# Low parts on VectorE, high parts by way of PSUM: one edit to the back phase of a fused attention and two-MLP kernel

## The chip, the core and the metric

The kernel runs on one core of a Trainium2 chip. The metric is the device time of one execution in microseconds (us), the median of three runs. Five engines work side by side: TensorE (PE, with its weight loads PEld), VectorE (DVE), ScalarE (ACT), GpSimd (POOL) and SyncE (SP), whose queue issues all the transfers here. Each works through its own instructions in order and waits for the others by semaphores.

## The reference

Windowed attention over (4, 8, 576, 64) gives 2304 tokens of width 512; two MLPs follow. The edit touches the second MLP only.

```python
def _moe_ref(x, w_in, w_out):          # first MLP, d_ff 2048
    h = x @ w_in
    g = h * np.cos(h)
    return (g @ w_out).astype(np.float32)

def _moe2_ref(x, w_a, w_b, w_out):     # second MLP, d_ff 1536
    a = x @ w_a
    b = x @ w_b
    return (a * b @ w_out).astype(np.float32)
```

## The kernel before, in words

**Precision.** Each fp32 operand is split in two: a high part, an ACT copy into the type that PE takes, and a low part, the fp32 value minus the high part, made by DVE or POOL. `mm3` then issues three matmuls: high by high (L430), high by low (L431), low by high (L432).

**The second MLP** runs after the attention and the first MLP. The 2304 tokens go in three groups (`GROUPS`) of 768. Each product of matrices is done as a 2x2 block scheme with seven block products P1 to P7 instead of eight. Its operand on the token side is one of seven blocks, named in `RHS`: P1 takes B11, P6 takes T2, P2 takes B21, P7 takes T3, P5 takes T1, P4 takes T4, P3 takes B22. T1 to T4 are sums of blocks and are made by POOL (`g_sum` for the back phase, `x_sum` for the projections). A group has 126 items, counted by `k`; `q` is its place in the group.

- **Projections**, q = 0 to 83: six pairs p of columns, 14 items each (P1, P6 for `a`, the same for `b`, P2, P7 for `a`, ... in the list `prods`). An item is two `mm3`, six matmuls of 384 columns. Results stand in PSUM banks `z`; DVE adds them up, multiplies `a` by `b` and leaves the blocks B11 to B22 in tiles `g` and `gp`.
- **Back phase**, q = 84 to 125 (r = q - 84 = 0 to 41): `a*b` times `w_out`. The seven products come in the order P1, P6, P2, P7, P5, P4, P3, six items each, so P1 is r = 0 to 5, P6 is 6 to 11, P2 is 12 to 17. Every item needs the high and low part of one block of `a*b` (`gh`, `gl`). `split_g(k + LG)` writes them into the queues LG = 6 items ahead of their use.

**What sets the order.** The main loop over `k` issues, in this order: weight loads (`fetch`), splits of the weights six items ahead (`stage`, tiles `sb`), `split_g`, the tasks of `xitems` (loads, sums and splits of the next group's input, tiles `xb`, `xh`, `xl`, `xw`, `xq`), the tasks of `soon` (`g_sum` and others), then the item itself. `InOrder` keeps ACT, DVE and POOL in the order of writing. So a late sum in POOL's queue holds up what stands behind it in ACT's and in DVE's.

**Which engine makes a low part** in the back phase is in the table `GDS`, one number for each product: (3, 3, 0, 2, 2, 3, 3) sends every third, every third, none, every second, ... to POOL, 14 of the 42 items of a group.

**PSUM** has eight banks in two sets of four, the tags `att`, `h` and `acc0` to `acc3`. `banks()` hands out the sets in turn: one to each pair of the projections, one to the back phase. During the back phase the other set is idle.

**`ev()`** hands out eight SBUF buffers in a ring for intermediate sums; `pair()` takes one of the 33 buffers `w` that the weight loads use as well. In the profile all instructions that `InOrder` records, that is all of the second MLP on ACT, DVE and POOL, have line L64.

Of the kernel before, what the change touches and what calls it, by code (L numbers as in the profile page):

```python
# [9 lines left out]
F32 = mybir.dt.float32  # L10
F32R = mybir.dt.float32r
# [4 lines left out]
AF = mybir.ActivationFunctionType  # L16
ALU = mybir.AluOpType
# [3 lines left out]
NT, DM = B * S, H * D  # L21
# [34 lines left out]


class InOrder:
    def __init__(self, tc, engine):
        self.tc, self.engine = tc, engine  # L60

    def __getattr__(self, name):
        f = getattr(self.engine, name)
        return lambda *a, **k: self.tc.keep_in_program_order(f(*a, **k))  # L64


@with_exitstack
def kernel(ctx, tc, qT, kT, vw, vds, w_in, w_out, w_a, w_b, w_out2, out):
    nc = tc.nc
    pe, act, dve, pool, sp = nc.tensor, nc.scalar, nc.vector, nc.gpsimd, nc.sync  # L70
# [5 lines left out]
    ps = ctx.enter_context(tc.tile_pool(name="ps", bufs=1, space=bass.MemoryType.PSUM))  # L76
# [350 lines left out]
    acc = {}  # L427
# [86 lines left out]
    if True:  # L514
# [181 lines left out]
        def x_sum(nm, j):  # L696
            if nm == "T3":
                t23 = pair("xb")
                xs["T2", j], xs["T3", j] = t23[:, 0], t23[:, 1]
            a, b = {"T3": ("B22", "T1"), "T1": ("T1", "B11"), "T2": ("B22", "T1"), "T4": ("B21", "T2")}[nm]  # L700
            pool.tensor_tensor(out=xs[nm, j], in0=xs[a, j], in1=xs[b, j], op=ALU.subtract)

        def x_hi(nm, j):
            if nm in ("B11", "T2", "T4", "B22"):
# [14 lines left out]

        J2 = [0, 1]  # L720
        xsteps = {5: [(load_x, 0, j) for j in J2]}
        for i, nm in ((7, "T3"), (8, "T1"), (9, "T2"), (12, "T4")):
            xsteps.setdefault(i, []).extend((x_sum, nm, j) for j in J2)
        for i, nm in ((8, "B11"), (9, "B21"), (10, "T3"), (11, "T1"), (12, "T2")):
            for f, at_ in ((x_hi, i), (x_lo, i + 1)):
                xsteps.setdefault(at_, [])[:0] = [(f, nm, j) for j in J2]
        xitems = {}
        for i, (nm, j) in enumerate([("T4", 0), ("T4", 1), ("B22", 0), ("B22", 1)]):
            xitems.setdefault((0, 1 + i), []).append((x_hi, nm, j))
            xitems.setdefault((0, 2 + i), []).append((x_lo, nm, j))  # L730

        def x_plan(G, r0):
            for j in J2:
                xitems.setdefault((G - 1, r0 - 14 + j), []).append((load_x, G, j))
                for r, nm in ((2, "T3"), (14, "T1"), (18, "T2"), (24, "T4")):
                    xitems.setdefault((G - 1, r0 + r + 2 * j), []).append((x_sum, nm, j))
                for r, nm in ((-6, "B11"), (-2, "B21"), (2, "B22"), (8, "T3"), (20, "T1"), (24, "T2"), (30, "T4")):
                    xitems.setdefault((G - 1, r0 + r + 2 * j), []).append((x_hi, nm, j))
                    xitems.setdefault((G - 1, r0 + r + 2 * j + 1), []).append((x_lo, nm, j))

        p2 = None
        for g in range(NG + LAG):
            if g < NG:
                i, u, f = seq[g]
                if g == NG - NF:
                    at_ctx.close()
                    p2 = ctx.enter_context(tc.tile_pool(name="p2", bufs=1))
                    act, dve, pool = InOrder(tc, act), InOrder(tc, dve), InOrder(tc, pool)
# [52 lines left out]
        def split_g(k):  # L801
            if k >= len(items) or items[k][0] != "back":
                return
            _, G, what, p = items[k]
            t = gt[RHS[what], p]
            r = k % PERI - NPR
            for d, tag in ((gh, "gh"), (gl, "gl")):
                if r % 2 and r < NP * len(AB) - 8:
                    d[k] = p2.tile([128, N2], F32R, tag="sb", name=tag, bufs=8)
                else:  # L810
                    d[k] = tmp.tile([128, N2], F32R, tag=tag, name=tag, bufs=C["NGH"])
            act.activation(out=gh[k], in_=t, func=AF.Copy)
            every = C["GDS"][AB.index(what)]
            (pool if every and p % every == every - 1 else dve).tensor_tensor(out=gl[k], in0=t, in1=gh[k].bitcast(F32), op=ALU.subtract)
            if what == "P2":
                gt["T4", p] = t
                soon.setdefault(k - LG + 2, []).append((g_sum, "T4", "B21", "T2", p))

        zlast = [None]
        seg = [0]  # L820

        def banks():
            s = seg[0] % 2
            seg[0] += 1
            names = (("att", 2), ("h", 2)) * 2 if s == 0 else tuple((f"acc{m}", 1) for m in range(4))
            return [ps.tile([128, N2], F32, tag=tag, name="z", bufs=n) for tag, n in names]

        def gtile(nm, p):
            if nm in ("B12", "B22"):
                gt[nm, p] = p2.tile([128, N2], F32, tag="g2", name="g2", bufs=12)  # L830
            else:
# [11 lines left out]
        def product(k, G, p, i):  # L843
# [40 lines left out]
            if not own and done:  # L884
                a = st["a"][done]
                dve.tensor_tensor(out=a, in0=a, in1=c[done], op=ALU.mult)
            if not own and what == "P3":
                gt["T1", p] = gt["B12", p]
                for d, nm, x, y in ((3, "T3", "B22", "T1"), (4, "T1", "T1", "B11"), (5, "T2", "B22", "T1")):
                    soon.setdefault(k + d, []).append((g_sum, nm, x, y, p))  # L890

        def g_sum(nm, x, y, p):
            dst = gt[nm, p] if nm in ("T1", "T4") else gtile(nm, p)
            pool.tensor_tensor(out=dst, in0=gt[x, p], in1=gt[y, p], op=ALU.subtract)

        def put(G, m, h, t):
            s0 = GROUPS[G] + N2 * h
# [61 lines left out]
        for k, it in enumerate(items):  # L959
# [78 lines left out]
```

## Time and profile before

| | |
|---|---|
| median of three runs | 988.29 us (987.73 to 989.37) |
| the profiled execution | 987.76 us, of which 985.6 us lie between its first and last instruction (the span) |
| PE, PEld busy | 942.4 us (96%), 892.4 us (91%) |
| DVE, ACT, POOL busy | 708.1 us (72%), 609.9 us (62%), 477.5 us (48%) |
| granted TensorE clock, mean | 0.979 of full speed |

The profiled execution is 0.53 us below the median. A sum that is made against the profile is therefore raised by that to be compared with a median. PE's busy time is modelled (its matmuls overlap), so what an item costs is better read from the distance of starts.

### The profile page before, as it was taken

How to read it: one execution, taken by the hardware profiler on the slowest of the kernel's cores; microseconds unless marked ns; L12 is line 12 of the kernel's file. 1: busy time of each engine (PE TensorE's matmuls, PEld its weight loads, DVE VectorE, ACT ScalarE, POOL GpSimd, SP SyncE). 2: the span in 40 equal slices, each digit the busy share in tenths (PEclk: the TensorE clock that was granted, in tenths of full speed). 3: DMA queues.
4: the chain of work that ended last, by engine and by line, in shares of the span. 5: the costliest groups of instructions: out<-in, count | busy, mean ns of one | idle time of the engine just before them, and what ended most of it. 6: DMA issues, size and time to landing. Idle time of an engine off the chain costs nothing.

```text
span 985.6 us, 18933 instructions
## 1 busy us (share of the span) xinstructions
PE 942.4 (96%) x6828; PEld 892.4 (91%) x6828; DVE 708.1 (72%) x1378; ACT 609.9 (62%) x1399; POOL 477.5 (48%) x615
## 2 busy tenths in 40 slices
PE   4888899999999999999999999999999999999998
PEld 3767898989889989899999989998999998999998
DVE  7677777577767777656346878889856789667773
ACT  5689897476675858676468765555444455444452
POOL 3757642014221351112015347658777769566682
PEclk8779999999999999999999999999999999999999
DMA  9646511244546363432049855576554685753431
GB/s 287 244 132 209 189 43 39 69 126 138 157 125 184 116 185 113 123 105 60 1 138 280 253 181 193 188 288 238 222 173 154 205 340 214 256 176 141 160 134 49
DMA packets 98829, 163.30 MB, mean 166 GB/s; under 512 B 6960, under 2 KB 64816, under 8 KB 98736
## 3 DMA queue, kind: packets, MB, share of 16 engines
q1 hardware_dynamic: 98736, 162.10, 49.7%
q8 instruction: 54, 0.88, 0.4%
q14 instruction: 39, 0.32, 0.1%
HBM read 128.25 MB, written 33.82 MB: 164 GB/s over the span
## 4 chain that ended last, share of the span: by engine, by line
PE 73%; DVE 10%; ACT 6%; DMA 5%; POOL 4%; issue 2%; SPq 0%; POOLq 0%; DVEq 0%; ACTq 0%
PE z L431 12%; PE z L432 12%; PE z L430 12%; PE h L430 5%; PE acc L430 5%; PE h L431 5%; PE h L432 5%; PE acc L432 5%; PE acc L431 5%; DMA vs<-in_vds_dram 2%; PE att L336 2%; PE att L217 1%; PE att L244 1%; POOL vd L183 1%; PE att L329 1%
## 5 line engine op out<-in xcount | busy, mean ns | idle before, releaser
L64 POOL TENSOR_TENSOR sb<-w,sb 128x256 fp32r<-128x256 f32 x154 | 120.7, 796 | 90.7 <-ACT sb L64 87.0
L430 PE MATMUL h<-xh,w 128*128 128x288 f32 (+1 forms) x448 | 146.7, 327 | 7.9 <-DVE gs L478 7.0
L430 PE MATMUL acc<-gh,w 128*128 128x288 f32 (+1 forms) x448 | 145.0, 325 | 2.0 <-DVE ev L463 1.0
L431 PE MATMUL acc<-gl,w 128*128 128x288 f32 (+1 forms) x448 | 142.3, 318 | 1.9 <-POOL gl L486 1.7
L432 PE MATMUL h<-xh,w 128*128 128x288 f32 (+1 forms) x448 | 142.1, 317 | 1.2 <-POOL w L126 1.2
L431 PE MATMUL h<-xl,w 128*128 128x288 f32 (+1 forms) x448 | 142.9, 319 | 0.0
L432 PE MATMUL acc<-gh,w 128*128 128x288 f32 (+1 forms) x448 | 141.9, 317 | 0.0
L64 ACT ACTIVATE sb<-w 128x256 fp32r<-128x256 f32 x252 | 96.4, 415 | 66.1 <-PE z L432 54.2
L430 PEld LDWEIGHTS h<-xh,w 128*128 128x128 f32 x448 | 85.6, 191 | 15.5 <-DVE gs L478 9.9
L432 PE MATMUL z<-xh,sb 128*128 128x384 f32 x288 | 97.4, 338 | 0.2 <-POOL sb L64 0.2
L430 PE MATMUL z<-xh,sb 128*128 128x384 f32 x288 | 96.9, 336 | 0.4 <-issue 0.4
L431 PE MATMUL z<-xl,sb 128*128 128x384 f32 x288 | 97.2, 338 | 0.0
L430 PEld LDWEIGHTS acc<-gh,w 128*128 128x128 f32 x448 | 85.1, 190 | 7.7 <-issue 2.9
L618 POOL TENSOR_TENSOR praw<-praw 128x128 f32<-128x128 f32 x24 | 12.8, 531 | 162.3 <-DVE praw L118 128.5
L431 PE MATMUL z<-gl,w 128*128 128x384 f32 x252 | 85.7, 340 | 4.4 <-DVE gl L64 4.1
L431 PEld LDWEIGHTS acc<-gl,w 128*128 128x128 f32 x448 | 85.2, 190 | 4.0 <-POOL gl L486 2.1
L432 PEld LDWEIGHTS h<-xh,w 128*128 128x128 f32 x448 | 86.0, 192 | 2.8 <-POOL w L126 1.5
L431 PEld LDWEIGHTS h<-xl,w 128*128 128x128 f32 x448 | 85.8, 192 | 1.9 <-issue 0.9
L432 PEld LDWEIGHTS acc<-gh,w 128*128 128x128 f32 x448 | 85.0, 190 | 2.4 <-issue 1.1
L430 PE MATMUL z<-gh,w 128*128 128x384 f32 x252 | 85.1, 338 | 0.1
L432 PE MATMUL z<-gh,w 128*128 128x384 f32 x252 | 84.9, 337 | 0.0
L64 DVE TENSOR_TENSOR sb<-w,sb 128x256 fp32r<-128x256 f32 x98 | 62.2, 637 | 26.5 <-ACT sb L64 26.4
(141 smaller groups left out, 2503.6 us busy)
## 6 DMA issues: line engine op xcount, KB each, us to landing
w<-wd SPq DMA_DIRECT2D x63, 512.0 KB
w<-wd_a SPq DMA_DIRECT2D x18, 512.0 KB
w<-wd_b SPq DMA_DIRECT2D x18, 512.0 KB
raw<-in_w_in_dram SPq DMA_DIRECT2D x16, 512.0 KB
raw<-in_w_out_dram SPq DMA_DIRECT2D x16, 512.0 KB
w<-wd_a SPq DMA_DIRECT2D x18, 384.0 KB
w<-wd_b SPq DMA_DIRECT2D x18, 384.0 KB
praw<-in_w_a_dram SPq DMA_DIRECT2D x12, 512.0 KB
```

The costliest lines, as they stand in the source:

```text
L64: return lambda *a, **k: self.tc.keep_in_program_order(f(*a, **k))
L183: pool.tensor_tensor(out=o, in0=t[:, :, 0], in1=t[:, :, 1], op=ALU.add)
L217: pe.matmul(p[r, W * w:W * w + W], qt[u, hp][r, off:off + W], kt[b, hp][r, BASE[half] + off:BASE[half] + off + W], start=not pem, stop=True,)
L244: pe.matmul(p[a][:QD, :SD], qd[u, hp][r, :], kd[b, hp][r, :], start=True, stop=True)
L329: pe.matmul(p[64 * a:64 * a + 64, NB:NB + QD], vdt[b, hp][:, a, c], pd[u, hp][:, 2 * a + c], start=(c == 0), stop=(c == 1),)
L336: pe.matmul(p[64 * a:64 * a + 64, xo:xo + n], vt[u, hp // 2][r, w, a], pt[u, hp // 2][r, w, 64 * a + qo:64 * a + qo + n], start=True, stop ...
L430: i = pe.matmul(ps_out, lh, rh, start=start, stop=False, skip_group_check=more)
L431: pe.matmul(ps_out, lh, rl, start=False, stop=False, skip_group_check=more)
L432: pe.matmul(ps_out, ll, rh, start=False, stop=stop, skip_group_check=more)
L618: pool.tensor_tensor(out=s1, in0=a21, in1=a22, op=ALU.add)
```

## The change

**In the back phase** `GDS` goes: DVE makes all low parts of P6 to P3, 36 for each group. For odd p (up to r = 38, which makes 16 for each group) ACT first copies the high part into a PSUM bank of the idle set (tile `hq`), and DVE subtracts that instead of the copy in SBUF. The matmuls take `gh` from SBUF as before.

**P1's splits move.** Its operand B11 is complete in the projections after P2 of `b`. It now stands in an `ev()` buffer, and its high and low part are made two and three items later (`b11_hi`, `b11_lo`) into a pair `gq`; for odd p POOL makes the low part, for even p DVE.

**The sums are ordered anew.** T2 is T3 + B11 instead of B22 - T1, so it comes before T1. Those of the last pair follow 1, 2 and 3 items after their last input instead of 3, 4 and 5. **The next group's input** is loaded at r = 0 instead of r = -14, its sums stand at r = 14 to 32 instead of 2 to 26, and its splits run from r = 6 to 47, the last ones in the next group's projections (before: -6 to 33). `InOrder` is written in another way and keeps the same order.

```diff
+SUMS = {"T3": ("B22", "T1", ALU.subtract), "T2": ("T3", "B11", ALU.add), "T1": ("T1", "B11", ALU.subtract),
+        "T4": ("B21", "T2", ALU.subtract)}
...
-                xitems.setdefault((G - 1, r0 - 14 + j), []).append((load_x, G, j))
-                for r, nm in ((2, "T3"), (14, "T1"), (18, "T2"), (24, "T4")):
-                for r, nm in ((-6, "B11"), (-2, "B21"), (2, "B22"), (8, "T3"), (20, "T1"), (24, "T2"), (30, "T4")):
+                put_x(G - 1, r0 + j, load_x, G, j)
+                for r, nm in ((14, "T3"), (18, "T2"), (24, "T1"), (30, "T4")):
+                for r, nm in ((6, "B11"), (12, "B21"), (24, "T2"), (28, "T3"), (33, "T1"), (39, "B22"), (44, "T4")):
...
+            if what == "P1":
+                gh[k], gl[k] = gsplit[p]
+                return
...
             act.activation(out=gh[k], in_=t, func=AF.Copy)
-            every = C["GDS"][AB.index(what)]
-            (pool if every and p % every == every - 1 else dve).tensor_tensor(out=gl[k], in0=t, in1=gh[k].bitcast(F32), op=ALU.subtract)
+            hi = gh[k].bitcast(F32)
+            if p % 2 and r < NP * len(AB) - 3:
+                tag, n = BANKS[seg[0] % 2][nst[1] % 4]
+                nst[1] += 1
+                hi = ps.tile([128, N2], F32, tag=tag, name="hq", bufs=n)
+                act.copy(out=hi, in_=gh[k].bitcast(F32))
+            dve.tensor_tensor(out=gl[k], in0=t, in1=hi, op=ALU.subtract)
...
+                if done == 11:
+                    soon.setdefault(k + 2, []).append((b11_hi, p))
+                    soon.setdefault(k + 3, []).append((b11_lo, p))
             if not own and what == "P3":
                 gt["T1", p] = gt["B12", p]
-                for d, nm, x, y in ((3, "T3", "B22", "T1"), (4, "T1", "T1", "B11"), (5, "T2", "B22", "T1")):
+                for d, nm in ((3, "T3"), (4, "T2"), (5, "T1")) if p < NP - 1 else ((1, "T3"), (2, "T2"), (3, "T1")):
...
+        def b11_hi(p):
+            q = pair("gq", F32R)
+            gsplit[p] = q[:, 0], q[:, 1]
+            act.activation(out=q[:, 0], in_=gt["B11", p], func=AF.Copy)
+
+        def b11_lo(p):
+            hi, lo = gsplit[p]
+            (pool if p % 2 else dve).tensor_tensor(out=lo, in0=gt["B11", p], in1=hi.bitcast(F32), op=ALU.subtract)
```

What POOL does around the start of the first group's back phase, before the change: the sums of the last pair of columns (`gp<-g,g` T3, `g<-g,gp` T1, `gp<-g,g` T2) stand among low parts `gl` and sums `xb` for the next group.

```order
L64 TENSOR_TENSOR gl<-gp,gh 128x384 x3
L64 TENSOR_TENSOR xb<-xb 128x384
L64 TENSOR_TENSOR gp<-g_8395,g_8343 128x384
L64 TENSOR_TENSOR g_8343<-g_8343,gp 128x384
L64 TENSOR_TENSOR xb<-xb 128x384
L64 TENSOR_TENSOR gp<-g_8395,g_8343 128x384
L64 TENSOR_TENSOR gl<-gp,gh 128x384
L64 TENSOR_TENSOR gp<-gp 128x384 x5
```

The same place of POOL's queue after the change (`gp<-gp,ev` is T2 = T3 + B11, `gq` the low part of B11 for the last pair, `gp<-gp` the six sums T4):

```order
L938 TENSOR_TENSOR gq<-ev,gq 128x384
L929 TENSOR_TENSOR gp<-g_8405,g_8352 128x384
L929 TENSOR_TENSOR gp<-gp,ev 128x384
L929 TENSOR_TENSOR g_8352<-g_8352,ev 128x384
L929 TENSOR_TENSOR gp<-gp 128x384 x6
L717 TENSOR_TENSOR xb<-xb 128x384 x8
```

All low parts have left POOL; T2 is the second of three sums that follow one another, and the sums for the next group stand behind all of the block sums.

DVE at the same place before the change: adds and multiplies of the last pair (`z`, `g`, `gp`), low parts, and low parts for the next group's input (`xl`, `xw`), mixed.

```order
L64 TENSOR_TENSOR gl<-gp,gh 128x384
L64 TENSOR_TENSOR g_8343<-g_8343,z 128x384
L64 TENSOR_TENSOR xw<-xb,xw 128x384
L64 TENSOR_TENSOR z<-ev,z 128x384
L64 TENSOR_TENSOR g_8343<-g_8343,z 128x384
L64 TENSOR_TENSOR gl<-gp,gh 128x384 x2
L64 TENSOR_TENSOR xw<-xb,xw 128x384
L64 TENSOR_TENSOR gl<-gp,gh 128x384
L64 TENSOR_TENSOR xl<-xb,xh 128x384
```

And after it, from the same multiply on:

```order
L872 TENSOR_TENSOR g_8352<-g_8352,z 128x384
L872 TENSOR_TENSOR z<-ev,z 128x384
L917 TENSOR_TENSOR g_8352<-g_8352,z 128x384
L842 TENSOR_TENSOR gl<-gp,gh 128x384
L842 TENSOR_TENSOR gl<-gp,hq 128x384
L842 TENSOR_TENSOR gl<-gp,gh 128x384
L842 TENSOR_TENSOR gl<-gp,hq 128x384
```

The low parts that follow the last multiply are now P6's, every second one with the PSUM operand `hq`; P1's and the next group's are gone from between the adds.

ACT at the same place after the change; a copy `hq` stands behind every second `gh`, and the two copies `ev<-z` wait for PE's end of P1:

```order
L934 ACTIVATE gq<-ev 128x384
L835 ACTIVATE gh<-gp 128x384 x2
L841 COPY hq<-gh 128x384
L835 ACTIVATE gh<-gp 128x384 x2
L841 COPY hq<-gh 128x384
L835 ACTIVATE gh<-gp 128x384 x2
L841 COPY hq<-gh 128x384
L963 COPY ev<-z 128x384 x2
```

Before it, `xh` and `xw` for the next group's input stood in the place of the copies `hq`.

## Rows read from the trace of the kernel before

**Rows 1.** Busy time by stage: projections and back phase of the three groups.

```profile
575.70:665.65 89.95, 89.08 (x505) 88.47 (x505) 77.13 (x138) 50.84 (x126) 58.39 (x71) 1.00 0.57 202
665.65:713.16 47.51, 45.22 (x253) 44.00 (x253) 44.72 (x54) 24.35 (x55) 38.03 (x32) 1.00 0.63 233
713.16:801.57 88.41, 88.41 (x506) 88.41 (x505) 61.61 (x113) 41.76 (x107) 64.20 (x79) 1.00 0.62 210
801.57:849.12 47.55, 45.25 (x253) 44.08 (x253) 44.71 (x54) 24.35 (x55) 38.05 (x32) 1.00 0.58 210
849.12:937.72 88.60, 88.60 (x506) 88.60 (x505) 61.63 (x114) 40.66 (x103) 57.40 (x71) 1.00 0.54 191
937.72:982.12 44.40, 44.40 (x253) 44.08 (x252) 25.86 (x36) 18.74 (x38) 24.82 (x21) 1.00 0.21 80
```

**Rows 2.** PE's waits in these stages: us in total, times, longest.

```profile
PE z L431 <- DVE gl L64: 4.1, 4, 1.3
PE z L431 <- POOL gl L64: 0.3, 2, 0.2
```

**Rows 3.** PE in order of time, first back phase: the two long waits.

```profile
683.55 0.44 PE L431 MATMUL z<-gl,w 128*128 128x384 f32 x1 [0.71 <-DVE gl L64]
...
687.55 0.44 PE L431 MATMUL z<-gl,w 128*128 128x384 f32 x1 [1.32 <-DVE gl L64]
```

**Rows 4.** ACT in order of time, ahead of these waits.

```profile
675.25 0.53 ACT L64 ACTIVATE gh<-gp 128x384 fp32r<-128x384 f32 x1 [5.23 <-POOL gp L64]
```

**Rows 5.** POOL in order of time, ahead of that wait of ACT.

```profile
668.47 1.34 POOL L64 TENSOR_TENSOR xb<-xb 128x384 f32<-128x384 f32 x1
670.07 1.27 POOL L64 TENSOR_TENSOR gp<-g,g 128x384 f32<-128x384 f32 x1 [0.26 <-DVE g L64]
...
672.59 1.34 POOL L64 TENSOR_TENSOR xb<-xb 128x384 f32<-128x384 f32 x1
673.89 1.33 POOL L64 TENSOR_TENSOR gp<-g,g 128x384 f32<-128x384 f32 x1
```

**Rows 6.** DVE in order of time in the first back phase.

```profile
667.62 1.32 DVE L64 TENSOR_TENSOR xw<-xb,xw 128x384 fp32r<-128x384 f32 x1
...
669.44 0.55 DVE L64 TENSOR_TENSOR g<-g,z 128x384 f32<-128x384 f32 x1
...
682.13 1.83 DVE L64 TENSOR_TENSOR gl<-gp,gh 128x384 fp32r<-128x384 f32 x2
683.88 1.37 DVE L64 TENSOR_TENSOR xw<-xb,xw 128x384 fp32r<-128x384 f32 x1
685.18 1.00 DVE L64 TENSOR_TENSOR ev<-ev,z 128x384 f32<-128x384 f32 x2
```

**Rows 7.** One low part of DVE and one of POOL, each without the other.

```profile
707.69 0.56 DVE L64 TENSOR_TENSOR gl<-g,gh 128x384 fp32r<-128x384 f32 x1 [0.90 <-ACT gh L64]
...
706.64 1.02 POOL L64 TENSOR_TENSOR gl<-g,gh 128x384 fp32r<-128x384 f32 x1 [3.07 <-ACT gh L64]
```

**Rows 8.** DVE's groups of the first back phase: busy us, mean ns.

```profile
L64 DVE TENSOR_TENSOR gl<-gp,gh 128x384 fp32r<-128x384 f32 x18 | 18.3, 1053 | 0.0
...
L64 DVE TENSOR_TENSOR ev<-ev,z 128x384 f32<-128x384 f32 x9 | 4.6, 545 | 0.8 <-PE z L432 0.8
```

**Rows 9.** POOL's groups of the first back phase.

```profile
L64 POOL TENSOR_TENSOR xb<-xb 128x384 f32<-128x384 f32 x8 | 10.6, 1331 | 0.0
L64 POOL TENSOR_TENSOR gl<-gp,gh 128x384 fp32r<-128x384 f32 x7 | 8.8, 1255 | 2.8 <-ACT gh L64 2.8
```

**Rows 10.** ACT's groups of the first back phase.

```profile
L64 ACT ACTIVATE gh<-gp 128x384 fp32r<-128x384 f32 x22 | 10.7, 522 | 11.3 <-PE z L432 5.6 <-POOL gp L64 5.2 <-PE z L431 0.4
...
L64 ACT COPY ev<-z 128x384 f32<-128x384 f32 x4 | 1.8, 476 | 2.3 <-PE z L432 2.2
```

**Rows 11.** Busy time at the start of the second group's projections.

```profile
713.20:728.00 14.80, 14.80 (x86) 14.80 (x85) 8.55 (x18) 6.61 (x17) 10.01 (x14) 1.00 0.40 120
```

**Rows 12.** PE in order of time, first projections: P5 of `b`, first pair.

```profile
586.53 0.44 PE L430 MATMUL z<-xw,sb 128*128 128x384 f32 x1 [0.67 <-DVE gp L64]
```

In Rows 1 and 11 the columns are: the stretch in us from the span's start, its length, then for PE, PEld, DVE, ACT and POOL the busy us and (x) the number of instructions, the granted clock, the share of the transfer engines and GB/s. In rows in order of time they are: start and duration in us, engine, line, operation, output and inputs, and in brackets the idle time before it and what ended that.

More of the change, by code (lines that the diff above doesn't have):

```diff
@@ L58, with __init__, written, settle @@
 class InOrder:
[L59 to L64, printed above, removed]
+    def __init__(self, tc, engines):
+        self.tc = tc
+        self.last = {e.engine: None for e in engines}
+        self.seen = len(self.written())
+    def written(self):
+        return self.tc.nc.cur_bb.bb.instructions
+    def settle(self):
+        for ins in self.written()[self.seen:]:
+            if ins.engine in self.last:
+                if self.last[ins.engine] is not None:
+                    self.tc.add_manual_dep(
+                        ins, self.last[ins.engine],
+                        mybir.DependencyInfo(mybir.DependencyClass.NoSync, mybir.DependencyReason.DATA),
+                        reason="program order")
+                self.last[ins.engine] = ins.name
+        self.seen = len(self.written())
 @with_exitstack
@@ L699, in x_sum @@
                 xs["T2", j], xs["T3", j] = t23[:, 0], t23[:, 1]
-            a, b = {"T3": ("B22", "T1"), "T1": ("T1", "B11"), "T2": ("B22", "T1"), "T4": ("B21", "T2")}[nm]
-            pool.tensor_tensor(out=xs[nm, j], in0=xs[a, j], in1=xs[b, j], op=ALU.subtract)
+            a, b, op = SUMS[nm]
+            pool.tensor_tensor(out=xs[nm, j], in0=xs[a, j], in1=xs[b, j], op=op)
         def x_hi(nm, j):
@@ L721 @@
         xsteps = {5: [(load_x, 0, j) for j in J2]}
-        for i, nm in ((7, "T3"), (8, "T1"), (9, "T2"), (12, "T4")):
+        for i, nm in ((7, "T3"), (8, "T2"), (9, "T1"), (12, "T4")):
             xsteps.setdefault(i, []).extend((x_sum, nm, j) for j in J2)
-        for i, nm in ((8, "B11"), (9, "B21"), (10, "T3"), (11, "T1"), (12, "T2")):
+        for i, nm in ((8, "B11"), (9, "B21"), (10, "T3"), (11, "T2"), (12, "T1")):
             for f, at_ in ((x_hi, i), (x_lo, i + 1)):
@@ L747 @@
                     p2 = ctx.enter_context(tc.tile_pool(name="p2", bufs=1))
-                    act, dve, pool = InOrder(tc, act), InOrder(tc, dve), InOrder(tc, pool)
+                    order = InOrder(tc, (act, dve, pool))
                 h_mm(g, u, f)
@@ L812, in split_g @@
             act.activation(out=gh[k], in_=t, func=AF.Copy)
-            every = C["GDS"][AB.index(what)]
-            (pool if every and p % every == every - 1 else dve).tensor_tensor(out=gl[k], in0=t, in1=gh[k].bitcast(F32), op=ALU.subtract)
+            hi = gh[k].bitcast(F32)
[5 more added lines that the diff above has]
+            dve.tensor_tensor(out=gl[k], in0=t, in1=hi, op=ALU.subtract)
             if what == "P2":
                 gt["T4", p] = t
-                soon.setdefault(k - LG + 2, []).append((g_sum, "T4", "B21", "T2", p))
+                soon.setdefault(k - LG + 2, []).append((g_sum, "T4", p))
         zlast = [None]
         seg = [0]
+        BANKS = ((("att", 2), ("h", 2)) * 2, tuple((f"acc{m}", 1) for m in range(4)))
         def banks():
@@ L824, in banks @@
             seg[0] += 1
-            names = (("att", 2), ("h", 2)) * 2 if s == 0 else tuple((f"acc{m}", 1) for m in range(4))
-            return [ps.tile([128, N2], F32, tag=tag, name="z", bufs=n) for tag, n in names]
+            return [ps.tile([128, N2], F32, tag=tag, name="z", bufs=n) for tag, n in BANKS[s]]
         def gtile(nm, p):
@@ L830, in gtile @@
                 gt[nm, p] = p2.tile([128, N2], F32, tag="g2", name="g2", bufs=12)
+            elif nm == "B11":
+                gt[nm, p] = ev()
             else:
@@ L886, in product, with g_sum @@
                 dve.tensor_tensor(out=a, in0=a, in1=c[done], op=ALU.mult)
+                if done == 11:
+                    soon.setdefault(k + 2, []).append((b11_hi, p))
+                    soon.setdefault(k + 3, []).append((b11_lo, p))
             if not own and what == "P3":
                 gt["T1", p] = gt["B12", p]
-                for d, nm, x, y in ((3, "T3", "B22", "T1"), (4, "T1", "T1", "B11"), (5, "T2", "B22", "T1")):
-                    soon.setdefault(k + d, []).append((g_sum, nm, x, y, p))
-        def g_sum(nm, x, y, p):
+                for d, nm in ((3, "T3"), (4, "T2"), (5, "T1")) if p < NP - 1 else ((1, "T3"), (2, "T2"), (3, "T1")):
+                    soon.setdefault(k + d, []).append((g_sum, nm, p))
+        def g_sum(nm, p):
+            x, y, op = SUMS[nm]
             dst = gt[nm, p] if nm in ("T1", "T4") else gtile(nm, p)
-            pool.tensor_tensor(out=dst, in0=gt[x, p], in1=gt[y, p], op=ALU.subtract)
+            pool.tensor_tensor(out=dst, in0=gt[x, p], in1=gt[y, p], op=op)
+        def b11_hi(p):
[5 more added lines that the diff above has]
+            (pool if p % 2 else dve).tensor_tensor(out=lo, in0=gt["B11", p], in1=hi.bitcast(F32), op=ALU.subtract)
+        gsplit = {}
         def put(G, m, h, t):
@@ L979 @@
                 back2(k, *it[1:])
+        order.settle()
 _INS = ["qT", "kT", "vw", "vds", "w_in", "w_out", "w_a", "w_b", "w_out2"]
```

11 lines of the change are left out of this document (7 added, 4 removed).

## The prediction

> **What bounds the kernel now.** I read the stages of the second MLP first. The six stretches of [rows 1] are projections and back phase of three groups that do the same matmuls. The first two back phases take 47.51 and 47.55 us, the third 44.40. In the third PE has no gap: 252 matmuls in 44.40 us are 0.176 us each, the step of the gapless projections too (504 in 88.41). The first two are thus 3.11 and 3.15 us too long, 6.26 together, and this is what an edit of the back phase can win. The third group has no next input to prepare, and DVE is busy 25.86 us in it against 44.72 and 44.71.
>
> PE's waits say what is late: low parts, 4.1 us of them DVE's in four waits and 0.3 POOL's [rows 2]; the restart of the matmul pipeline behind each gap makes up the rest of the 6.26. The two long waits of the first group end at 683.55 and 687.55 [rows 3]. The second group repeats them at the same distance from its start, so nothing random is in it.
>
> Why a low part is late is read from the queues ahead of it. ACT sat 5.23 us until 675.25 behind a POOL sum [rows 4]. That sum is T2 of the last pair. POOL reached it last of three, after low parts and with two sums `xb` for the next group between: T3 at 670.07, an `xb` at 672.59, T2 at 673.89 [rows 5]. DVE then had a train of low parts at double price. One alone took 0.56 us, one of POOL alone 1.02 [rows 7]; while both engines run, the same forms take 1.3 to 1.4 on either [rows 6, 9], and DVE's mean in the phase is 1053 ns [rows 8]. DVE's adds with one PSUM operand keep to 545 ns in the same phase [rows 8]. So two engines that each read two SBUF tiles get in each other's way, and a PSUM operand takes DVE out of it.
>
> **The change part by part.** Prices: two adds in a row took 1.00 us, one alone 0.55, so DVE's step is 0.45 to 0.47 us; I use 0.47. The `xw` at 683.88 was followed by the next instruction at 685.18, a step of 1.30 [rows 6]. A collision thus costs DVE about 0.82 us.
>
> *DVE in the first two back phases.* By the new order it has there 36 low parts, 11 low parts of the next input, 13 adds and multiplies and 2 weight splits: 62 instructions, 29.1 us at 0.47. POOL has 3 + 6 block sums and 8 sums `xb`, 17 in all. No POOL instruction can hit more than about one of DVE's, so collisions add at most 17 x 0.82 = 13.9: 43.0 us, under the 44.4 that PE needs. As a cross-check, before it is 54 instructions: 25.4 us, and the measured 44.72 leaves 19.3, that is 24 collisions with POOL's 32 instructions [rows 1]. Of the 62, 16 low parts and the 13 adds and multiplies read PSUM; I expect some 10 collisions, 37 us. In the third group DVE gets 12 low parts more and P1's fewer, POOL keeps 9 sums, and DVE had 18.5 us to spare [rows 1].
>
> For `hq` as an operand the trace has no low part. The adds (545 ns, one PSUM operand) and the lone low part (0.56, two SBUF operands) are the nearest rows [rows 7, 8], and they agree, so 0.47 stands. [...]
>
> *The first waits.* The multiply that ended at 669.99 on DVE stood behind an `xw` [rows 6]; without it, and leaving P1's low parts uncounted, it ends by 668.75. Up to the low part that PE missed first (r = 16, wanted at 682.5, just ahead of [rows 3]) DVE now has 11 low parts, 5 of them with `hq`, and 2 of the next input. If all eight that read SBUF alone collide: 8 x 1.29 + 5 x 0.47 = 12.7, ready at 681.4, still in time; POOL has far fewer than eight instructions to run there. ACT must have T2's high part by then. POOL's three sums now follow one another from about the same input, at 1.27 to 1.33 each [rows 5], so T2 is ready about 670 to 671 instead of 675.2. Behind that, each low part is queued six items ahead, 6 x 6 x 0.176 = 6.3 us.
>
> *ACT* gets 16 copies `hq` for each group. No row shows ACT writing PSUM. Nearest are 476 ns from PSUM to SBUF and 522 from SBUF to SBUF [rows 10]; in a train the 55 instructions of the phase averaged 0.44 [rows 1]. I take 0.5 and keep 0.4 to 0.8. In the 36 items in which splits are made (38 us) ACT has 50 other instructions, 22 us, so a copy may cost up to 1.0 us before ACT is the bound. Each copy stands ahead of the next `gh`; the first also waits until DVE has emptied the other bank set, which it does with the multiplies that the low parts follow anyway.
>
> *P1's splits* are 6 high parts on ACT and 6 low parts for each group, before and after. Before, they were issued in the last six items of the projections, 4 low parts to DVE and 2 to POOL; now each follows its pair of columns, 3 and 3. DVE has 27 us to spare in the second and third, 12.8 in the first [rows 1]. Their cover is the gap of two or three items between a DVE result and PE's next use of the bank. Without cover each costs 0.47 to 1.29; for the nine on DVE that is 4.2 to 11.6 us. I take 0.3 for all, since the first group is tight at its start, where PE already waits 0.67 us for DVE's multiply [rows 12], and `gq` stands behind that multiply.
>
> *The next input.* Four low parts (B22, T4) now fall into the first items of the next projections, at most 4 x 1.29 = 5.2 us on DVE, which was busy 8.55 of 14.80 there [rows 11]; T4 is first wanted ten items in, five after its low part. Its loads are issued some 15 items later but still 6 ahead of the first split, with the transfer engines at 0.63 [rows 1]. Both are costed at nothing; a miss would cost about 1 us for each boundary, 2 in all. The order of T2 and T1 and the form of `InOrder` cost nothing: the number of sums stays.
>
> **Sum.** -6.26 + 0.3 = -5.96 against the profiled 987.76: 981.8. That execution is 0.53 below the median, so 982.3 for a median. PE, with its unchanged matmuls, remains the bound.
>
> **The rivals.**
> *Only half goes.* From r = 34 on all high parts share one ring of four buffers, so the lead falls from six items to three or four (3.2 us), and DVE has three low parts of the next input there. If PE waits there, or the second long wait stays, about half is won: 988.3 - 3.1 = 985.2. Against it: that shortage was there before too, and no wait of [rows 3] lies there; POOL is idle then.
> *Nothing goes.* The change might not do what it says: if `hq` did not keep DVE clear of POOL and ACT came late by the copies, the waits would move from r = 16 to other items: 988.0. The bound of 43.0 does not need `hq` at all, which speaks against it.
> *Slower.* P1's low parts on DVE come out in the open in the projections, at the hand-over from DVE's reading a bank to PE's reusing it, as once in [rows 12]. With 1.29 each for nine, 988.3 - 6.3 + 11.6 = 993.6; slower from 0.7 us each on. Against it: only the first group shows such a wait, and only one, with DVE at 77.13 of 89.95 us; the others have DVE at 61.6 of 88.5 [rows 1].
>
> **How the numbers follow.** The forecast has 0.76, half 0.09, nothing 0.09, slower 0.06. About 0.2% (2 us) is what a measurement of this kernel tells from no change. Half is still faster by 0.3%: faster 0.85, same 0.09, slower 0.06. The forecast's own range runs from 980.8 (all of the 6.26 and the wait of [rows 12] and its like in the first projections, another 1.2) to 984 (the 2 us at the boundaries); to hold eight in ten I take it up to the half case, 986.
>
> **What would show it.** Right: the first two back phases last 44.4 to 45 us with no wait of `z` for `gl` over 0.3; DVE is busy 35 to 41 us in each; low parts with `hq` take 0.55 beside a busy POOL; copies `hq` take 0.4 to 0.6; T2 of the last pair is done by 671. The projections stay within 0.5 us of [rows 1]. Wrong: PE waiting for DVE `ev` or `gq` inside the projections, for ACT `hq` ahead of a low part, or for `xl` at the start of a group; or `hq` copies over 1 us.

## The result and the profile after

| | before | after |
|---|---|---|
| median of 10 runs | 989.15 us (984.14 to 993.35) | 979.94 us (977.28 to 985.18) |
| ratio after to before | | 0.991, 95% interval 0.988 to 0.993 |
| the profiled execution, its span | 987.76, 985.6 us | 977.28, 975.4 us |

The change is faster by 0.9%. The median lies 2.4 us below the forecast of 982.3 and 0.9 us below the range. The ten runs of before have a median 0.86 us above that of the three runs that the forecast started from, so the medians differ by 9.2 us where the forecast had 6.0.

The stages of the second MLP after the change (columns as in [rows 1]):

```profile
572.86:661.86 89.00, 88.82 (x504) 88.50 (x505) 72.85 (x138) 49.23 (x123) 59.76 (x72) 1.00 0.59 208
661.86:706.04 44.18, 44.18 (x254) 44.18 (x254) 35.59 (x58) 32.74 (x73) 23.33 (x21) 1.00 0.62 232
706.04:794.63 88.59, 88.59 (x505) 88.59 (x505) 65.46 (x118) 40.58 (x106) 66.95 (x80) 1.00 0.62 216
794.63:838.75 44.12, 44.12 (x253) 44.12 (x253) 35.57 (x58) 32.79 (x73) 23.31 (x20) 1.00 0.59 221
838.75:927.25 88.50, 88.50 (x505) 88.50 (x505) 64.54 (x118) 41.84 (x106) 60.03 (x72) 1.00 0.51 179
927.25:971.59 44.34, 44.34 (x253) 44.01 (x252) 25.96 (x47) 26.16 (x54) 10.64 (x9) 1.00 0.30 115
```

Against [rows 1] the first two back phases are 3.33 and 3.43 us shorter, and PE has no gap left in them: 252 matmuls in 44.18 us are 0.1753 us each, the step of the projections before (504 in 88.41). The third phase gained 0.06. The projections changed by -0.95, +0.18 and -0.10. The six stages together lost 7.68 us (406.41 to 398.73, from the first matmul's start). The second MLP also began earlier, at 572.86 instead of 575.72 (2.86 us), behind code that the change leaves alone but for the order of a few of the first group's input sums and splits close to its end.

PE's waits for the second MLP after the change, all that the view lists:

```profile
PE z L444 <- issue: 0.4, 1, 0.4
PE z L446 <- POOL sb L819: 0.2, 1, 0.2
```

The waits for `gl` of [rows 2] are gone. The groups of DVE and ACT in the first back phase:

```profile
L842 DVE TENSOR_TENSOR gl<-gp,gh 128x384 fp32r<-128x384 f32 x12 | 11.2, 936 | 1.7 <-ACT gh L835 1.7
L842 DVE TENSOR_TENSOR gl<-gp,hq 128x384 fp32r<-128x384 f32 x12 | 6.6, 546 | 3.2 <-ACT hq L841 3.2
...
L872 DVE TENSOR_TENSOR ev<-ev,z 128x384 f32<-128x384 f32 x8 | 4.0, 546 | 0.0
...
L835 ACT ACTIVATE gh<-gp 128x384 fp32r<-128x384 f32 x22 | 11.3, 520 | 4.3 <-PE z L446 1.9 <-POOL gp L929 1.9 <-DVE gl L842 0.4
L841 ACT COPY hq<-gh 128x384 f32<-128x384 f32 x16 | 7.7, 484 | 5.2 <-DVE g L872 4.7
```

A low part that reads `hq` takes 546 ns, to the nanosecond what the adds with a PSUM operand take; with `gh` the mean of these twelve is 936. DVE and POOL in order of time, where both are busy:

```profile
679.41 1.37 DVE L842 TENSOR_TENSOR gl<-gp,gh 128x384 fp32r<-128x384 f32 x1
680.70 0.54 DVE L842 TENSOR_TENSOR gl<-gp,hq 128x384 fp32r<-128x384 f32 x1
...
677.74 10.39 POOL L717 TENSOR_TENSOR xb<-xb 128x384 f32<-128x384 f32 x8
```

The hand-over from the projections, phase start 661.86: DVE's last multiply of the last pair, POOL's T3 and T2, and ACT's wait for T2.

```profile
662.66 0.55 DVE L917 TENSOR_TENSOR g<-g,z 128x384 f32<-128x384 f32 x1
...
663.29 1.26 POOL L929 TENSOR_TENSOR gp<-g,g 128x384 f32<-128x384 f32 x1 [6.09 <-DVE g L917]
664.63 1.22 POOL L929 TENSOR_TENSOR gp<-gp,ev 128x384 f32<-128x384 f32 x1
...
665.88 0.53 ACT L835 ACTIVATE gh<-gp 128x384 fp32r<-128x384 f32 x1 [1.90 <-POOL gp L929]
```

Counted from the start of the phase, the multiply ends at 1.35 us (before at 4.34 [rows 6]), T2 at 3.99 (before at 9.57 [rows 5]).

### The profile page after: what moved, and what is told of

It is laid out like the page before. It is cut to its first block, busy times and chain, and to the rows that moved or that the text cites. A ratio compares the mean times of both kernels' runs of the same rounds, so it can differ in the third digit from the quotient of the medians.

```text
span 975.4 us, 18988 instructions
## 1 busy us (share of the span) xinstructions
PE 937.6 (96%) x6828; PEld 890.0 (91%) x6828; DVE 692.2 (71%) x1411; ACT 632.3 (65%) x1447; POOL 440.2 (45%) x582
## 4 chain that ended last, share of the span: by engine, by line
PE 77%; DVE 7%; ACT 6%; DMA 4%; POOL 3%; issue 3%; SPq 0%; DVEq 0%; POOLq 0%; ACTq 0%
PE z L446 14%; PE z L445 14%; PE z L444 14%; PE h L444 5%; PE acc L444 5%; PE h L445 5%; PE h L446 5%; PE acc L445 5%; PE acc L446 5%; PE att L350 2%; DMA vs<-in_vds_dram 2%; PE att L231 1%; PE att L258 1%; POOL vd L197 1%; PE att L343 1%
## 5 line engine op out<-in xcount | busy, mean ns | idle before, releaser
L819 POOL TENSOR_TENSOR sb<-w,sb 128x256 fp32r<-128x256 f32 x154 | 124.7, 824 | 109.8 <-ACT sb L817 108.3
L632 POOL TENSOR_TENSOR praw<-praw 128x128 f32<-128x128 f32 x36 | 18.6, 517 | 233.4 <-DVE praw L132 192.8
L492 DVE SCALAR_TENSOR_TENSOR gs<-gs,h 128x288 f32<-128x288 f32 (+1 forms) x112 | 55.2, 493 | 50.1 <-ACT gs L491 49.8
L483 ACT ACTIVATE gs<-h 128x288 int32<-128x288 f32 (+1 forms) x112 | 49.3, 440 | 49.1 <-PE h L446 48.1
L484 DVE SCALAR_TENSOR_TENSOR gs<-gs,h 128x288 f32<-128x288 int32 (+1 forms) x112 | 55.1, 492 | 32.6 <-ACT gs L483 32.2
```

The costliest lines, as they stand in the source:

```text
L483: act.activation(out=k, in_=hps[g], func=AF.Copy, scale=1.0 / (2.0 * math.pi))
L484: dve.scalar_tensor_tensor(out=gs[g], in0=k, scalar=-2.0 * math.pi, in1=hps[g], op0=ALU.mult, op1=ALU.add)
L492: dve.scalar_tensor_tensor(out=s, in0=s, scalar=1.0, in1=hps[g], op0=ALU.subtract, op1=ALU.mult, reverse0=True)
L632: pool.tensor_tensor(out=s1, in0=a21, in1=a22, op=ALU.add)
L819: (dve if nst[0] % (C["SD"] if G else C["SD0"]) == 0 else pool).tensor_tensor(out=t[:, 1], in0=blk, in1=t[:, 0].bitcast(F32), op=ALU.subtract)
```

## The experiments

The prediction's reason for the two long waits has two halves: T2 comes late in POOL's queue and holds ACT up [rows 4, 5], and DVE then has a train of low parts at double price. The rival that grew out of the first runs: what is late is DVE's last multiply at the hand-over, behind P1's low parts and the next input's; all that follows is shifted by it, in a DVE queue that has no slack to make it up.

All of them are in one table. Phases are the first two back phases in us. "Multiply" and "T2" are the ends of the last pair's last multiply and of its T2, in us from the start of the first phase. "DVE in 22 us" is its busy time in the first 22 us of that phase, in which both long waits of [rows 3] end, with the number of instructions. "Low part r = 18" is the one that PE's longest wait in [rows 3] is for: when it is done, in us from the start of the first phase, and in brackets the number of DVE instructions from that start up to and with it. A PE without a gap takes it 19.08 us after the start (after).

| kernel | ratio to before (95%) | phases | multiply | T2 | DVE in 22 us | low part r = 18 |
|---|---|---|---|---|---|---|
| before | 1 | 47.51, 47.55 | 4.34 | 9.57 | 21.93 (27) | 21.85 (26) |
| after | 0.991 (0.988 to 0.993) | 44.18, 44.12 | 1.35 | 3.99 | 18.55 (27) | 16.33 (19) |
| after_again | 0.993 (0.990 to 0.996) | 44.17, 44.12 | 1.35 | 3.99 | 18.56 (27) | 16.33 (19) |
| p1_only | 0.995 (0.992 to 0.997) | 44.73, 44.60 | 1.50 | 6.70 | 21.96 (24) | 19.02 (21) |
| p1_back | 0.993 (0.991 to 0.996) | 44.22, 44.22 | 2.06 | 4.70 | 19.42 (30) | 16.40 (22) |
| x_late_only | 0.994 (0.992 to 0.996) | 45.26, 45.35 | 1.34 | 6.83 | 17.05 (22) | 17.34 (18) |
| sums_only | 1.003 (1.000 to 1.005) | 48.43, 48.43 | 3.60 | 6.25 | 21.93 (26) | 22.77 (26) |
| t2_first | 1.000 (0.998 to 1.002) | 47.51, 47.56 | 4.35 | 6.99 | 21.93 (27) | 21.86 (26) |
| split_only | 0.997 (0.995 to 0.999) | 45.98, 45.84 | 3.81 | 9.03 | 20.03 (31) | 20.75 (28) |
| split_no_hq | 0.998 (0.996 to 1.001) | 47.83, 46.06 | 3.83 | 9.05 | 21.93 (29) | 21.44 (28) |
| split_sums | 0.995 (0.992 to 0.997) | 44.22, 44.25 | 3.36 | 6.00 | 21.96 (35) | 17.58 (27) |
| no_hq | 0.996 (0.993 to 0.998) | 45.62, 45.59 | 1.35 | 3.99 | 20.73 (24) | 16.13 (19) |
| pool_lows | 0.991 (0.988 to 0.994) | 44.53, 44.10 | 1.35 | 3.98 | 19.83 (22) | 16.14 (17) |

**The change once more** (after_again, no edit).

> The changed kernel once more, unchanged, to see how much of its gain stands outside the second MLP. Profile so far: second MLP 398.7 us against 406.4 before, and 2.9 us more ahead of it, in code that no edit touched. If that part comes from the granted clock of the run (0.86 and 0.89 in two stretches of the first MLP before, 1.00 there after), the second MLP lasts 398.7 +- 0.4 again, the part ahead of it is off by up to 3 us either way, and the ratio is 0.991 to 0.994. Rival: the edit moved something ahead of the second MLP; then its start is again near 572.9 us.

Its median was 982.75 us (978.85 to 987.61), its ratio 0.993. The back phases repeat to 0.01 us, the first projections do not:

```profile
575.78:665.87 90.09, 89.33 (x504) 88.37 (x505) 74.02 (x138) 49.07 (x123) 59.75 (x72) 1.00 0.58 206
665.87:710.04 44.17, 44.17 (x253) 44.17 (x253) 35.61 (x58) 32.75 (x73) 23.34 (x20) 1.00 0.61 230
```

The second MLP takes 399.8 us here, 6.6 less than before, and starts at 575.78. So of the 10.2 us between the two spans, the start (2.86) and some 1.1 of the first projections did not come again.

**P1's splits alone, and put back** (p1_only: before with this; p1_back: after without it, all six low parts of P1 on DVE).

```diff
+            if what == "P1":
+                gh[k], gl[k] = gsplit[p]
+                return
...
+                if done == 11:
+                    soon.setdefault(k + 2, []).append((b11_hi, p))
+                    soon.setdefault(k + 3, []).append((b11_lo, p))
```

> The kernel before with P1's splits alone moved into the projections. Input theory: the input's work still stands ahead of T2 and of the low parts of P6 and P2, back phases 46.5 to 47.5 us. P1 theory: 44.2 to 45.5 us.

> The changed kernel with P1's splits put back to six items ahead of use (all six low parts on DVE). Input theory: the start of the phase still has room, back phases 44.1 to 44.8 us. P1 theory: 45.5 us or more.

Alone, this edit wins 2.78 and 2.95 us in the two phases, 5.7 of the 6.8 that all parts win together. DVE's last multiply, POOL's T2 and ACT behind it, phase start 666.56:

```profile
667.51 0.55 DVE L64 TENSOR_TENSOR g<-g,z 128x384 f32<-128x384 f32 x1
...
671.94 1.32 POOL L64 TENSOR_TENSOR gp<-g,g 128x384 f32<-128x384 f32 x1
...
673.30 0.53 ACT L64 ACTIVATE gh<-gp 128x384 fp32r<-128x384 f32 x1 [8.37 <-POOL gp L64]
```

The multiply ends 2.84 us earlier than before. T2 is done 2.87 us earlier too; ACT's wait for it is longer than before, 8.37 us against 5.23 [rows 4], since P1's splits no longer stand ahead of it. What PE needed came just in time. The low part of r = 18 on DVE, in before and here:

```profile
686.11 1.39 DVE L64 TENSOR_TENSOR gl<-gp,gh 128x384 fp32r<-128x384 f32 x1
...
684.16 1.42 DVE L64 TENSOR_TENSOR gl<-gp,gh 128x384 fp32r<-128x384 f32 x1
```

It is done 21.85 us after the phase start before, 2.77 too late, and 19.02 here, 0.06 ahead of PE, with 21 DVE instructions up to it instead of 26. PE has no long wait any more. The projections that took the splits in lasted 89.93, 88.38 and 88.63: nothing. Putting the splits back into the full change costs 0.04 and 0.10 us, so with the other parts there this one is not needed.

**T2 earlier** (sums_only: the change's order of block sums, with the last pair's two items earlier; t2_first: T2 second of the three, distances as before).

```diff
-                for d, nm, x, y in ((3, "T3", "B22", "T1"), (4, "T1", "T1", "B11"), (5, "T2", "B22", "T1")):
+                for d, nm, x, y in ((3, "T3", "B22", "T1"), (4, "T2", "T3", "B11"), (5, "T1", "T1", "B11")):
-                    soon.setdefault(k + d, []).append((g_sum, nm, x, y, p))
+                    soon.setdefault(k + (d if p < NP - 1 else d - 2), []).append((g_sum, nm, x, y, p))  # sums_only
...
-            pool.tensor_tensor(out=dst, in0=gt[x, p], in1=gt[y, p], op=ALU.subtract)
+            pool.tensor_tensor(out=dst, in0=gt[x, p], in1=gt[y, p], op=ALU.add if nm == "T2" else ALU.subtract)
```

> The kernel before with the order of the block sums alone changed: T2 = T3 + B11 ahead of T1, those of the last pair two items earlier. Everything else, P1's splits, POOL's low parts, the early input, as before. Queue theory: T2 of the last pair is done by 672, ACT's wait of 5.2 us goes, the two long waits of PE (0.7 and 1.3 us) shrink to under 0.5 and the back phases to 45 us, so -4 to -5 us. Collision theory: DVE is as busy (44 to 45 us) and late as before, waits stay or move by some items, within 2 us of the kernel before.

> Before with one edit: T2 = T3 + B11 and stands second of the three block sums instead of third (distances 3, 4, 5 as before), so that it comes one to three POOL instructions earlier (8.3 to 6.9 us after the start of the phase instead of 9.6) without POOL standing idle for DVE's multiply any longer than before. If the lateness of T2 in POOL's queue is what made the two long waits, the first two back phases shrink by 1 to 2.5 us each (45 to 46.5 instead of 47.5) and the whole by 2 to 5 us, ratio 0.995 to 0.998. If it is the crowd on DVE behind the last multiply, at double price, they stay at 47.2 to 47.8 and the ratio is 1.000 +- 0.002; ACT's wait for T2 would be 2 to 4 us instead of 5.2 all the same.

In t2_first T2 is done 2.58 us sooner and ACT's wait for it halves. PE's first long wait moves from r = 16 to r = 10 (0.48 us instead of 0.71); the second stays where it was, as long as it was, and so does the phase's length:

```profile
672.28 1.21 POOL L64 TENSOR_TENSOR gp<-gp 128x384 f32<-128x384 f32 x1
...
673.52 0.53 ACT L64 ACTIVATE gh<-gp 128x384 fp32r<-128x384 f32 x1 [2.64 <-POOL gp L64]
...
677.85 0.44 PE L431 MATMUL z<-gl,w 128*128 128x384 f32 x1 [0.48 <-DVE gl L64]
...
688.42 0.45 PE L431 MATMUL z<-gl,w 128*128 128x384 f32 x1 [1.32 <-DVE gl L64]
```

A late T2 is thus not what made these waits by itself. DVE is busy 21.93 of the first 22 us with T2 early or late, and the low part of r = 18 is the 26th instruction of its queue in both, done at 21.85 and 21.86: ACT's work can come sooner and DVE cannot take it. In sums_only POOL stood 4.48 us before the first sum, which waited for DVE's multiply, with a low part of P6 queued behind, and PE then missed that:

```profile
671.98 1.27 POOL L64 TENSOR_TENSOR gp<-g,g 128x384 f32<-128x384 f32 x1 [4.48 <-DVE g L64]
...
681.04 0.44 PE L431 MATMUL z<-gl,w 128*128 128x384 f32 x1 [0.84 <-POOL gl L64]
```

**The low parts' engine and `hq`** (split_only: before with all low parts on DVE and `hq`; split_no_hq: the same without `hq`; no_hq: after without `hq`; pool_lows: after without `hq` and with `GDS` again for P6 to P3).

```diff
-            (pool if every and p % every == every - 1 else dve).tensor_tensor(out=gl[k], in0=t, in1=gh[k].bitcast(F32), op=ALU.subtract)
+            dve.tensor_tensor(out=gl[k], in0=t, in1=hi, op=ALU.subtract)   # hi: gh, or hq for odd p
```

> The kernel before with the low parts alone edited: all 42 on DVE, every second one of P6 to P3 with its high part copied to PSUM; P1's splits stay in their place. Input theory: POOL gets free sooner for T2, but DVE has 8 low parts more in the same crowded third; back phases 46 to 48 us. Collision theory: 44.2 to 45.5 us.

> Before with all 42 low parts of a back phase on DVE and no copies hq. With them the same edit gave back phases of 45.98 and 45.84 and DVE 39.4 us busy. If hq is what makes the move pay, these last 47.4 to 49 us each, DVE is busy 45 to 48, and the whole is as slow as before or slower (ratio 1.000 to 1.004). If emptying POOL is what pays, and hq only adds a little, 45.8 to 46.5 and ratio 0.996 to 0.998.

> The changed kernel without the copies hq: all low parts of P6 to P3 on DVE, from SBUF. Queue theory (what counted is that T2 of the last pair comes early and POOL has no low parts): back phases stay at 44.1 to 44.5 us, DVE busy there up to 43 instead of 37, time as the changed kernel within 0.5 us. Collision theory (the PSUM operand is what keeps DVE in time): PE waits for gl again, back phases 45.5 us or more in the first two groups.

> The changed kernel without hq and with POOL's share of the low parts of P6 to P3 given back (12 for each group); P1's move, the order of the sums and the late input stay. Queue theory: the early T2 alone is enough, back phases 44.1 to 45 us. Collision theory: POOL has 29 instructions in the phase again, DVE is busy 42 us or more and PE waits for low parts, back phases 46 to 47.5 us.

Within the full change the move is worth nothing: pool_lows has the same ratio as after, and phases that are 0.35 us longer and 0.02 shorter. Moved without `hq`, the low parts cost 1.45 us a phase (no_hq). DVE was busy 41.52 of 45.62 us there, under the bound of 43.0, but it met POOL's eight sums `xb` in one block with two-SBUF operands only, and PE missed one of the low parts (DVE, then PE, in order of time):

```profile
687.76 1.37 DVE L734 TENSOR_TENSOR xw<-xb,xw 128x384 fp32r<-128x384 f32 x1
689.05 2.66 DVE L837 TENSOR_TENSOR gl<-gp,gh 128x384 fp32r<-128x384 f32 x2
...
694.34 0.44 PE L445 MATMUL z<-gl,w 128*128 128x384 f32 x1 [0.50 <-DVE gl L837]
```

In the crowded phase of before the move alone wins 3.2 us over the two phases with `hq` and 1.2 without. Without `hq` the first phase lost 0.3 and the second gained 1.5, and the trace shows where. The same 28 DVE instructions were done at 21.44 us in the first phase and at 16.29 in the second. In the first DVE and POOL slowed each other as before: four low parts from 682.58 took 3.60 us, and POOL's four sums T4 beside them 5.14. In the second the same four, from 818.62, took 1.95, DVE kept its step of 0.47, and two of POOL's sums T4 took 4.09 and 3.77 us beside it (POOL and DVE, in order of time; the second phase starts at 807.55):

```profile
819.24 4.09 POOL L64 TENSOR_TENSOR gp<-gp 128x384 f32<-128x384 f32 x1 [2.84 <-DVE gl L64]
823.29 2.89 DVE L64 TENSOR_TENSOR gl<-gp,gh 128x384 fp32r<-128x384 f32 x6
823.29 3.77 POOL L64 TENSOR_TENSOR gp<-gp 128x384 f32<-128x384 f32 x1
```

What decides which engine is held up, the runs do not tell. Neither split_only nor split_no_hq fell clearly on one side of what was expected. With `hq` (split_only) DVE had 1.97 us free in the first 22, and one wait stayed; there T2 did come too late for it (ACT, then PE, in order of time):

```profile
677.98 0.53 ACT L64 ACTIVATE gh<-gp 128x384 fp32r<-128x384 f32 x1 [4.00 <-POOL gp L64]
...
689.72 0.44 PE L431 MATMUL z<-gl,w 128*128 128x384 f32 x1 [1.32 <-DVE gl L64]
```

**Both without the rest** (split_sums: split_only with the sums of sums_only).

> Before with all 42 low parts on DVE, hq for odd p, and the block sums of the change (T2 second, the last pair's two items earlier). The sums alone made the phases 0.9 us longer, with low parts of POOL queued behind a sum that waited for DVE's multiply. With no low part left on POOL that harm is gone: if an earlier T2 is worth something by itself, the first two back phases last 44.4 to 45.3 us instead of 45.9 and the long wait of 1.32 at r = 18 goes; if it is not, 45.7 to 46.2 with a wait of 1.0 to 1.4 for DVE gl in the same place.

The first two back phases, busy time by stage:

```profile
670.91:715.13 44.22, 44.22 (x253) 44.22 (x253) 39.31 (x65) 31.78 (x71) 24.76 (x21) 1.00 0.67 249
...
803.54:847.79 44.25, 44.25 (x254) 44.25 (x253) 39.17 (x65) 31.78 (x71) 24.77 (x21) 1.00 0.64 233
```

No gap, with P1's splits and the next input where they were before. The sums, worth nothing or less alone, win 1.6 to 1.8 us a phase once DVE has time to use an early T2 and POOL has no low part left behind them. DVE is again full, 21.96 of 22 us, but has done 35 instructions in it instead of 27.

**The next group's input alone** (x_late_only).

```diff
-                xitems.setdefault((G - 1, r0 - 14 + j), []).append((load_x, G, j))
+                put_x(G - 1, r0 + j, load_x, G, j)
...
-                for r, nm in ((-6, "B11"), (-2, "B21"), (2, "B22"), (8, "T3"), (20, "T1"), (24, "T2"), (30, "T4")):
+                for r, nm in ((6, "B11"), (12, "B21"), (24, "T2"), (28, "T3"), (33, "T1"), (39, "B22"), (44, "T4")):
```

> The kernel before with the next group's input alone moved: loaded at r = 0, sums at r = 14 to 32, splits at r = 6 to 47, T2 ahead of T1 among these. Input theory (DVE and POOL were late because the next group's sums and splits fell into the first third of the back phase, among P1's and P6's splits and the last block sums): back phases 44.2 to 45 us, -5 to -6.5 us. P1 theory (P1's six splits at the phase's start were what put DVE behind): back phases stay above 46.5. If it takes both: 45 to 46.5.

It wins 2.25 and 2.20 us: the multiply is again early (1.34), DVE has 5 us to spare in the first 22, and the low part of r = 18 is done at 17.34. What is left are two short waits in each of the two phases for POOL's low parts, 0.2 us each.

## Why the prediction was wrong

**The direction and the place were right.** What repeats of the gain is in the first two back phases, `z` no longer waits for `gl`, and none of the rivals came.

**The step that failed is the range's low end, by its terms.** It put 980.8 as all of the 6.26 of the back phases plus 1.2 of the first projections. It sized the gain of the back phases too small and gave the code ahead of the second MLP no width at all.
- *Back phases, -6.26 put, -6.82 measured.* The floor was read from the third phase, 44.40 [rows 1]. That phase is followed by no other, so its stretch runs to the end of its last matmul (0.34 us) and not to a next start; the gapless step of the projections, 0.1754 us, times 252 gives 44.2, and that is where the other two went (3.33 and 3.43 gained, and 0.06 in the third).
- *P1's splits, +0.3 put, 0.0 measured* (p1_only).
- *The first projections, -0.95 in the first profile, +0.14 in the repeat.* The stage's length goes with the place of DVE's second copy out of the first MLP. In the kernel before, this copy starts 0.51 us after the stage's start, and DVE's four weight splits, beside POOL's, then take 3.34. In after it starts at 1.99, held up by a store, the splits take 1.57, and the wait of [rows 12] is gone. In the repeat it starts at 2.69; the splits take 1.42 but come so late that PE waits 0.23 us for one, and 0.35 for a `g` further on. x_late_only, which moves no split of P1, has the copy at 1.84 and also 89.00 us. Why the copy's place differs, the runs do not tell. Two rows of after and, below, three of the repeat, DVE and PE in order of time:

```profile
574.85 0.61 DVE L477 COPY ev<-acc 128x432 f32<-128x432 f32 x1 [2.90 <-DMA y_dram<-ev]
575.38 1.57 DVE L819 TENSOR_TENSOR sb<-w,sb 128x256 fp32r<-128x256 f32 x4
...
578.47 0.61 DVE L477 COPY ev<-acc 128x432 f32<-128x432 f32 x1 [3.61 <-DMA y_dram<-ev]
579.00 1.42 DVE L819 TENSOR_TENSOR sb<-w,sb 128x256 fp32r<-128x256 f32 x4
579.47 0.44 PE L446 MATMUL z<-xh,sb 128*128 128x384 f32 x1 [0.23 <-DVE sb L819]
```
- *The code ahead of the edit* was given no term and no width. Over the 13 profiles its end, the start of the second MLP, lay between 572.86 (after) and 581.40 (split_no_hq), with 576.67 in the middle and 575.72 for before. The first profile of after is the earliest of all.

By the second MLP alone, 6.6 to 7.7 us from 987.76 with the 0.53 to a median, the change is worth 980.6 to 981.7, the low end of the range. The rest of the way to 979.94, 0.7 to 1.7 us, lies outside the second MLP, as the early start of the first profile does. The start did not come again in the repeat, whose series gave 982.75 against 990.80 for before, a ratio of 0.993 where the forecast has 0.994. What sets these starts stays open.

**The reason given for the long waits was half right.** "DVE's train of low parts at double price" stood: DVE was full in the first 22 us, and the low part of r = 18 was done 2.77 us after PE could take it. "T2 late in POOL's queue" was not what held it up (t2_first); it counts only once DVE has room, 1.6 to 1.8 us a phase from split_only to split_sums. What the prediction took for a side effect, the multiply behind an `xw`, belongs to the same queue: each single edit that brings the multiply to 1.3 to 1.5 us removes the long waits (p1_only, x_late_only), each that leaves it at 3.6 to 4.4 keeps one in the first phase (sums_only, t2_first, split_only, split_no_hq). But these two edits also take 5 and 8 instructions out of DVE's queue ahead of r = 18, and no run moves the multiply alone. So the work ahead of that low part is what the runs show, and a part of its own for the multiply is not shown. split_sums shows the other way out: the multiply still at 3.36, 27 instructions up to r = 18 instead of 26, and these done at 17.58 us, since they cost 0.65 each and not 0.84. The parts overlap: P1's splits, the next input and the low parts with `hq` win 5.7, 4.5 and 3.2 us alone, and all parts together 6.8.

**"The bound of 43.0 does not need `hq` at all"** held as a sum (41.52) and failed as an argument (no_hq, 0.50 of wait and 1.45 us): a bound over 44 us says nothing of a block of 10 us in which each low part costs 1.3.

**Smaller steps.** `hq` copies 0.48 us (0.5 taken); low parts with `hq` 0.546 (0.55), beside a busy POOL what a low part with two SBUF operands takes with POOL idle (0.55 at 688.56 in after), so the price by the rows was the right one; DVE busy 35.6 us (37 expected); T2 at 3.99 us after the phase start (4.4 to 5.4 expected, as 670 to 671); first waits gone. Four low parts of the next input in the next projections: nothing was put, and the second projections were 0.2 us longer in both profiles of the change and the third 0.1 shorter.

## What to carry to other kernels

When a queue is suspected, read the busy time of its engine in the stretch ahead of the wait, not in the whole stage: DVE was at 94% of the phase and at 99.7% of the 22 us that mattered. What counts in such a stretch is the work that stands in the queue ahead of what is wanted first, and what each piece of it costs: work that can be done earlier or later, standing at the hand-over between two stages, delays all that the next stage starts from. And a forecast of a fraction of a per cent needs a width for the code that is not touched, here over 8 us from the earliest to the latest start of the second MLP.

## What was not expected of the hardware

**The clock ahead of the edit.** Two stretches of the first MLP, before the change (columns as in [rows 1]):

```profile
110.00:140.00 30.00, 28.95 (x218) 27.40 (x217) 21.65 (x43) 26.71 (x64) 17.47 (x23) 0.94 0.38 122
...
260.00:290.00 30.00, 28.79 (x247) 27.13 (x245) 20.00 (x55) 23.39 (x53) 8.80 (x18) 0.94 0.48 145
```

And after it, the same code:

```profile
110.00:140.00 30.00, 28.85 (x224) 26.85 (x223) 21.54 (x43) 26.90 (x65) 17.80 (x24) 1.00 0.36 121
...
260.00:290.00 30.00, 28.85 (x274) 26.80 (x273) 20.20 (x55) 24.38 (x58) 8.59 (x20) 1.00 0.48 141
```

By these means, 0.94 and 1.00, before lost at most 0.06 x 30 = 1.8 us of full speed in each stretch, 3.6 in both, as an estimate; 2.86 us is what the second MLP began earlier. But the clock explains only a part of it. With ACT's instructions matched one by one, after is 0.38 us ahead at 121 us (times of before) and still 0.38 at 145, although the granted clock was 0.82 and 0.76 from 122 to 130. It is 0.67 ahead at 271 and 1.90 at 287, with 0.89 and 0.82 from 270 to 282: some 1.2 us there. Another 0.98 came between 344 and 364, at 1.00 in both. And split_no_hq, at 0.95 in the first 110 us where before and after had 0.84, began its second MLP latest of all. PE was busy 84.54 of these 110 us in both before and after, so the rows do not say why one lost clock and the other did not.

**A collision is paid by both engines, or by one.** In after eight sums `xb` took 10.39 us beside DVE's low parts, a step of 1.30, where a lone POOL instruction of this size took 1.02 [rows 7]; DVE's step with two SBUF operands is 0.83 (from 683.76) or 1.29 (from 679.41) there instead of 0.47 (from 688.56, POOL idle). Those with `hq` kept to 546 ns beside the same sums. One after the other, a lone sum and a lone step of DVE would be 1.02 + 0.47 = 1.49 for each of the eight, and measured is 1.30. In the second phase of split_no_hq DVE paid nothing and POOL 4.09 and 3.77 us for one sum.
